# Accumulating across PSUM bank pairs: the two row halves of the TensorE array swap banks halfway through a sum

## The chip, the cores and the metric

The kernel runs on 1 core of one Trainium2 chip. The metric is the device time of one execution in microseconds; lower is better. The kernel before was run three times (180.81, 182.23 and 182.66 us, median 182.23 us). One further execution was recorded by the hardware profiler; all rows of a profile in this text come from that one.

## What is computed

The reference is a sigmoid attention followed by a token-mixing MLP, for 8 batches, 12 heads, 448 positions and heads of 64:

```python
def _attn_ref(q, k, v):
    scores = scale * np.matmul(q, k.transpose(0, 1, 3, 2)) - np.log(S)
    attn = 1.0 / (1.0 + np.exp(-scores))
    return np.matmul(attn, v)
...
def _moe_ref(x, w_q, w_k, w_out):      # x: 8 x 448 x 768
    wq = x @ w_q                       # 448 x 64
    wk = x @ w_k                       # 448 x 64
    W_tok = scale * np.einsum('bsd,btd->bst', wq, wk)
    mixed = np.einsum('bst,btd->bsd', W_tok, x)
    return np.maximum(mixed, 0.0) @ w_out
```

The kernel never forms W_tok. It computes wk-transposed times x first (a 64 x 768 matrix for each batch) and then wq times that.

## The kernel before, in words

**Units of work.** The 96 pairs of batch and head are handled as 24 "quads" of four heads; three quads make one batch ("unit" u, 0 to 7). Everything is bf16 on TensorE and float32 in PSUM. PSUM has 8 banks, which the program takes singly or in pairs in the order that the string BANKS (L67) lists.

**Four tiles of the array.** Most matmuls use the 128 x 128 array as four 64 x 64 tiles that run side by side: two row halves (`y` or `g` or `h`, the upper or lower 64 partitions of the operands, thus which half of a contraction) times two column halves (`x`, the upper or lower 64 partitions of the result). A group of four such matmuls is what one step in the plan issues several times. Because the two row halves work at the same time, they write to different banks of a pair.

**The plan.** The order of all work is written out by hand as a string of letters, PLAN (L132), which the loop at L803 walks. Each letter issues one step, and each engine runs its own instructions in that order. The letters that matter:
- S (`scores`, L307): four matmuls of 448 columns for one of 168 blocks of keys into a bank pair; ScalarE then writes the sigmoid of both banks to one of 16 `at` buffers (L316).
- P (`values`, L326): four matmuls of 448 columns that add one such block to the attention output of a quad; after seven of them the result goes to the tile `xt` (L342, at the end or for R split between VectorE and ScalarE, L340).
- x, X (`tr_x`, L346): transposes of `xt` into `xn`, in 64 x 64 tiles (x, L371) or whole (X, L355).
- W, w, L, l (`mlp_wqk`, L389): six steps for each unit give wq and wk. W and w use the whole array and one bank (L408). L and l use the four tiles: row half y sums its half of the contraction into bank y over all 448 columns (L396), and at the end one bank is copied to a float32 tile (L403), then the other is added to it (L404). POOL copies wq to the other half of the partitions (L405 and L417, or ScalarE at L415).
- N (`mlp_wkn`, L419): wk is transposed. U, u, T, t (`mlp_tmp` L431, `mlp_tmp_tiled` L443): wk-transposed times x; the tiled form again has two half sums in two banks, a copy (L456) and an addition (L457).
- M, m, G (`mlp_mix`, L466): three steps for each unit, a ReLU into the tile `mx` (L461 on ScalarE, L463 on VectorE). For the middle four units (the pairs of units listed in TW, L129) the step issues eight matmuls of 256 columns (L476) and writes `mx` in a wider layout; for the others it issues four of 448 columns (L490).
- O, o, Q, I, i: the product with `w_out`. Two units make 7 chunks of 128 tokens, 28 chunks in all, and each chunk takes four steps. There are three forms. `out_chunk` (L585) uses the whole array, three matmuls of 384 columns in a step (L603); it serves 44 steps, among them the last 20. `out_halves` (L545) uses four tiles, 12 matmuls of 384 columns in a step (L562): one block of 64 tokens at a time, both halves of the contraction into two banks, then a copy (L567) and an addition (L568); 12 steps. `out_pair` (L510) uses four tiles too, 12 matmuls in a step (L522), 56 steps: row half y makes all of the sum for token block y in bank y, so nothing has to be added, but each row half needs all of `w_out` and of `mx` on its own 64 partitions. That is why `wout16` (L107) holds `w_out` twice, the second copy with the halves of the partitions exchanged, made by the steps C (12 DMAs on the SP queue, L848), and why TW has its own layout of `mx`.
- q, k, a to f, r, s, z: q and k are cast and transposed to the layout that S wants. POOL does most casts (L192, L209, L215) and the exchange of partition blocks for kind c (L161, L164, L167), VectorE the 32 x 32 transposes (L245, L269, L276). The order of casts and loads is the string ORDER (L688). 1 and 2 give a cast to VectorE or ScalarE. F is filler for TensorE at the start.

**Queues.** Loads of q, k and v and nearly all stores are issued by SP in order (L173, L179, L543, L576, L613). A load waits for one of 8 buffers, a store for its copy out of PSUM into one of 3 buffers `o` (L60).

**Waiting on TensorE.** Matmuls carry no waits on other matmuls. TensorE's only waits are on other engines: that a bank has been read, or that an operand is there.

## Time and profile before

| | us |
|---|---|
| median of three runs | 182.23 |
| the profiled execution: its own time | 181.22 |
| its span, first to last instruction | 179.4 |
| PE busy / DVE busy / ACT busy / POOL busy | 169.1 / 143.0 / 158.9 / 124.2 |

PE is TensorE's matmuls, PEld its weight loads, DVE VectorE, ACT ScalarE, POOL GpSimd, SP the engine whose queue issues most DMAs. The granted TensorE clock was 0.997 over the span. A matmul's row lasts from its first column to the arrival of its last result, and matmuls overlap each other, so that PE is shown as busy even where it could take more work. The chain of waits, which lists for each stretch only the piece that the next one had to wait for, shows how far apart the pieces really start.

### The profile page before, as it was taken

The page shows a single profiled execution, that of the slowest core. Times are in us where ns is not written, and L with a number is a line of the kernel's source. Part 1 is how long each engine was busy: PE and PEld are TensorE (multiplying, and loading weights), DVE is VectorE, ACT ScalarE, POOL GpSimd, SP SyncE. Part 2 cuts the span into 40 slices and gives each one's busy share as a digit, 9 for nine tenths or more (in the row PEclk, how much of TensorE's full clock was granted, in tenths as well). Part 3 has the DMA queues.
Part 4 walks back from the last instruction along what each step waited for, and adds up shares of the span by engine and source line. Part 5 has one row for each costly group of instructions (what it writes and reads, how often), then busy time and mean ns, then how long its engine had stood idle before and what let it go on. Part 6 is the DMA issues. An engine that isn't in the chain of part 4 may idle for free.

```text
span 179.4 us, 7848 instructions
## 1 busy us (share of the span) xinstructions
PE 169.1 (94%) x3412; PEld 115.5 (64%) x3412; DVE 143.0 (80%) x223; ACT 158.9 (89%) x208; POOL 124.2 (69%) x169
## 2 busy tenths in 40 slices
PE   7888899889999999999999999999999999999990
PEld 7334545444674555755667788787888788888560
DVE  3447899998988897989999989979799885868351
ACT  4699999999999999999999999999999989967310
POOL 1286899998999999999999989879979810010000
PEclk9999999999999999999999999999999999999998
DMA  5999999999999998899996999959597432505876
GB/s 166 338 398 391 326 383 377 285 305 365 335 309 406 334 287 280 249 319 384 306 325 174 303 313 302 331 207 274 130 325 219 115 89 49 137 4 128 207 195 175
DMA packets 24914, 47.29 MB, mean 264 GB/s; under 512 B 3888, under 2 KB 18480, under 8 KB 24880
## 3 DMA queue, kind: packets, MB, share of 16 engines
q1 hardware_dynamic: 23600, 44.64, 76.9%
q0 software_dynamic: 800, 1.18, 3.6%
q10 hardware_dynamic: 480, 0.98, 1.5%
q8 instruction: 26, 0.43, 1.0%
q14 instruction: 8, 0.07, 0.1%
HBM read 35.78 MB, written 11.01 MB: 261 GB/s over the span
## 4 chain that ended last, share of the span: by engine, by line
PE 76%; ACT 15%; DMA 4%; SPq 1%; issue 1%; POOL 1%; DVE 0%
PE banks L311 16%; ACT at L316 15%; PE banks L522 15%; PE banks L333 14%; PE banks L603 13%; DMA k<-in_k_dram 4%; PE banks L562 3%; PE banks L408 3%; PE banks L371 2%; PE banks L396 2%; PE banks L355 2%; PE banks L452 2%; PE banks L476 1%; PE banks L490 1%; PE banks L437 1%
## 5 line engine op out<-in xcount | busy, mean ns | idle before, releaser
L316 ACT ACTIVATE at<-banks 128x896 bf16<-128x896 f32 x168 | 139.9, 951 | 2.9 <-PE banks L311 2.3
L311 PE MATMUL banks<-qk 64*64 64x448 bf16 x672 | 62.6, 357 | 3.7 <-ACT at L316 1.7
L333 PE MATMUL banks<-at,v 64*64 64x448 bf16 x672 | 47.3, 350 | 0.7 <-ACT at L316 0.7
L311 PEld LDWEIGHTS <-qk 64*64 64x64 bf16 x672 | 26.3, 105 | 21.4 <-issue 13.5
L522 PE MATMUL banks<-wout,mx 64*64 64x384 bf16 x672 | 36.3, 323 | 0.0
L333 PEld LDWEIGHTS <-v 64*64 64x64 bf16 x672 | 24.8, 106 | 6.7 <-issue 1.8
L342 DVE CAST xt<-banks 128x896 bf16<-128x896 f32 x22 | 23.7, 1083 | 2.4 <-PE banks L333 2.0
L522 PEld LDWEIGHTS <-mx 64*64 64x64 bf16 x672 | 23.2, 107 | 3.9 <-issue 0.2
L603 PE MATMUL banks<-wout,mx 128*128 128x384 bf16 (+1 forms) x138 | 24.4, 320 | 0.0
L192 POOL CAST qk<-k 128x896 bf16<-128x896 f32 x19 | 22.7, 1194 | 1.4 <-DMA k<-in_k_dram 1.0
L192 POOL CAST qk<-q 128x896 bf16<-128x896 f32 x18 | 21.5, 1193 | 2.5 <-DVE qk L276 1.4
L463 DVE TENSOR_SCALAR mx<-banks 128x1024 bf16<-128x1024 f32 (+3 forms) x22 | 21.3, 970 | 1.9 <-PE banks L476 0.7
L209 POOL CAST v<-v 128x896 bf16<-128x896 f32 x22 | 20.6, 950 | 1.4 <-DMA v<-in_v_dram 0.9
L603 PEld LDWEIGHTS <-mx 128*128 128x128 bf16 x138 | 12.3, 98 | 9.7 <-issue 3.2
L161 POOL COPY swap<-qk 32x448 uint32<-32x448 uint32 x28 | 15.5, 554 | 2.3 <-DVE qk L192 0.7
L276 DVE STREAM_TRANSPOSE qk<-qk 128x448 f32<-128x448 f32 x28 | 17.0, 628 | 0.1
L164 POOL COPY qk<-qk 32x448 uint32<-32x448 uint32 x28 | 15.8, 566 | 1.6
L167 POOL COPY qk<-swap 32x448 uint32<-32x448 uint32 x28 | 15.4, 552 | 1.6
L245 DVE STREAM_TRANSPOSE qk<-qk 32x448 f32<-32x448 f32 x24 | 15.3, 636 | 0.6
L405 POOL COPY wq<-wqk 64x448 bf16<-64x448 bf16 x3 | 1.7, 554 | 15.7 <-DVE wqk L404 15.7
L636 DVE COPY o<-banks 128x384 f32<-128x384 f32 x12 | 6.6, 554 | 5.7 <-PE banks L603 5.3
L636 ACT COPY o<-banks 128x384 f32<-128x384 f32 x9 | 4.4, 490 | 7.1 <-PE banks L603 6.6
(87 smaller groups left out, 207.9 us busy)
## 6 DMA issues: line engine op xcount, KB each, us to landing
q<-in_q_dram SPq DMA_DIRECT2D x24, 448.0 KB, 6.6
v<-in_v_dram SPq DMA_DIRECT2D x24, 448.0 KB, 6.6
k<-in_k_dram SPq DMA_DIRECT2D x23, 448.0 KB, 7.6
out_dram<-o SPq DMA_DIRECT2D x50, 192.0 KB, 4.2
wout<-in_moe_w_out_dram POOLq DMA_DIRECT2D x2, 576.0 KB, 11.7
wout<-wout SPq DMA_DIRECT2D x12, 96.0 KB, 5.6
out_dram<-o ACTq DMA_DIRECT2D x4, 192.0 KB, 3.2
k<-in_k_dram SPq DMA_DIRECT2D x1, 256.0 KB, 4.8
```

The costliest lines, as they stand in the source:

```text
L161: eng.tensor_copy(out=z[lo], in_=w[hi, 0])
L164: eng.tensor_copy(out=w[hi, 0], in_=w[lo, 1])
L192: COPY[e](out=f[:, :, "qk".index(nm)].rearrange("p e i d y -> p e y i d"), in_=ld.pop((nm, n)).rearrange("p (y i e d) -> p e y i d", y=2, ...
L209: COPY[e](out=t16.rearrange("p b i d -> p (b i d)"), in_=ld.pop((nm, n)).rearrange("p b x -> p (b x)"),)
L276: nc.vector.transpose(out=qk[n][:, t].rearrange("p t i n -> p (t i n)").bitcast(F32), in_=w)
L311: nc.tensor.matmul(sc[HALF[h], g, 0:S], qk[n][HALF[g], h, 1, i, :], qk[n][HALF[g], h, 0].rearrange("p i n -> p (i n)"), start=True, stop=True,
L316: inst = nc.scalar.activation(at, sc[:, :, 0:S], ACTF.Sigmoid, bias=attn_bias, scale=attn_scale)
L333: nc.tensor.matmul(ps[HALF[g], h, 0:S], ld["v16", n][HALF[h], g, i, :], ats[n, i][HALF[h], g, :], start=(i == 0), stop=(i == NI - 1),)
L342: read(fb, COPY[eng](out=xt(u, j)[:, :, 0:S], in_=ps[:, :, 0:S]))
L463: inst = nc.vector.tensor_scalar(dst, ps, moe_scale, 0.0, ALU.mult, ALU.max)
L522: nc.tensor.matmul(ps[HALF[x], y, 0:NB], mx[HALF[y], u, b, 64 * (i - 3 * y) : 64 * (i - 3 * y) + 64], wout16[HALF[y], slot(y, b), x * NB : ...
L603: nc.tensor.matmul(ps, mxs[w][:, 2 * S * c + m * P : 2 * S * c + (m + 1) * P], wout16[:, c, w0:w1], start=(c == 0), stop=(c == NC - 1),)
```

## The change

- `wout16` holds `w_out` once; the steps C and their 12 DMAs are gone. `out_pair` and the TW forms of `mlp_mix` and `mx` are gone: every mix step issues four matmuls of 448 columns, and every chunk in tiles goes through `out_halves`.
- `out_halves` no longer adds. One bank pair holds a chunk of two token blocks. In the steps with part 0 and 1 row half y sums its half of the contraction for token block y in bank y. In parts 2 and 3 the halves have changed: row half y goes on with the other token block in the other bank, adding to what the other half left there. One copy (or a pair of copies on VectorE and ScalarE, letter J) takes both banks out.
- `mlp_wqk` in tiles does the same with the two halves of the 448 columns, in twice as many matmuls of 224 columns; step j of the first three takes both blocks of quad j, so step 2 already needs the unit's last quad. `mlp_tmp_tiled` does it with the two halves of 384 columns, in twice as many matmuls of 192, and its second half is a step of its own (V; for an untiled unit V does nothing).
- Between the two halves `change` puts a nop on TensorE's queue that waits for the last matmul before the change.
- 20 `at` buffers in place of 16, 4 `o` buffers in place of 3.
- The strings BANKS, PLAN and ORDER are all new. By letters the new plan has 72 output steps in tiles (18 chunks) and 40 whole ones (before 68 and 44), 18 tiled W steps (3 units) as before, 4 tiled units in T and 4 untiled (before 5 and 3), 9 X and 15 x (before 10 and 14), 13 quads of kind c and 7 of kind r (before 14 and 6).

```diff
-    p_o = pool("o", 3)
+    p_o = pool("o", 4)
...
+    SYNC = mybir.DependencyInfo(mybir.DependencyClass.Sync, mybir.DependencyReason.DATA)
+    turned = {}
+
+    def change(key):
+
+        tc.add_manual_dep(
+            nc.tensor.nop().ins, turned.pop(key).ins.name, SYNC, reason="the halves of the array change banks",
+        )
...
-    wout16 = singles.tile([P, 2 * NC, D], BF16, name="wout16")
+    wout16 = singles.tile([P, NC, D], BF16, name="wout16")
...
-    at_bufs = [singles.tile([P, 2, S], BF16, name=f"at{n}") for n in range(16)]
+    at_bufs = [singles.tile([P, 2, S], BF16, name=f"at{n}") for n in range(20)]
...
-    TW = (1, 2,)
...
+        w, w2 = wqks[u % 2], wq2s[u % 2]
         if tiled:
-            for y in range(2):
-                for x in range(2):
-                    nc.tensor.matmul(
-                        ps[HALF[x], y, 0:S], wqk16[HALF[y], c, 64 * x : 64 * x + 64],
-                        xt(u, c // 2)[HALF[y], c % 2, 0:S], start=(c == 0), stop=(c == NC - 1),
-                    )
+
+
+            z, j = divmod(c, NJ)
+            if c == NJ:
+                change("W")
+            for b in (2 * j, 2 * j + 1):
+                for y in range(2):
+                    for x in range(2):
+                        inst = nc.tensor.matmul(
+                            ps[HALF[x], y ^ z, 0 : S // 2], wqk16[HALF[y], b, 64 * x : 64 * x + 64],
+                            xt(u, j)[HALF[y], b % 2, (y ^ z) * S // 2 : (y ^ z) * S // 2 + S // 2],
+                            start=(z == b == 0), stop=(z == 1 and b == NC - 1),
+                        )
+            if c == NJ - 1:
+                turned["W"] = inst
             if c == NC - 1:
-                w, w2 = wqks[u % 2], wq2s[u % 2]
-                part = p_one.tile([P, S], F32, tag="wpart", name="wpart")
-                read(fb, COPY["s" if act else "v"](out=part, in_=ps[:, 0, 0:S]))
-                read(fb, nc.vector.tensor_tensor(out=w[:, 0:S], in0=ps[:, 1, 0:S], in1=part, op=ALU.add))
-                nc.gpsimd.tensor_copy(out=w2[HALF[1]], in_=w[HALF[0], 0:S])
+                src = ps[:, :, 0 : S // 2]
+                read(fb, nc.vector.tensor_copy(out=w[:, 0:S].rearrange("p (z s) -> p z s", z=2), in_=src))
+                if tail or act:
+                    read(fb, nc.scalar.copy(out=w2[HALF[1]].rearrange("p (z s) -> p z s", z=2), in_=src[HALF[0]]))
+                else:
+                    nc.gpsimd.tensor_copy(out=w2[HALF[1]], in_=w[HALF[0], 0:S])
...
-            w, w2 = wqks[u % 2], wq2s[u % 2]
...
-    def mlp_tmp_tiled(u, act):
-        tmps[u] = p_one.tile([P, NB], BF16, tag="tmp", name="tmp")
-        part = p_one.tile([P, NB], F32, tag="upart", name="upart")
-        fb, ps, _ = bank2()
+    def mlp_tmp_tiled(u, t, act):
+        h = NB // 2
+        if t == 0:
+            tmps[u] = p_one.tile([P, NB], BF16, tag="tmp", name="tmp")
+            pt[0] = bank2()
+        else:
+            change("T")
+        fb, ps, _ = pt[0]
+
         for m in range(4):
             for r in range(2):
                 if 2 * m + r == NI:
                     continue
+                z = r ^ t
                 for y in range(2):
-                    nc.tensor.matmul(
-                        ps[HALF[y], r, 0:NB], wkn[u][HALF[r], m, :], xns[u][HALF[r], m, y * NB : (y + 1) * NB],
-                        start=(m == 0), stop=(m == 3 - r),
+                    inst = nc.tensor.matmul(
+                        ps[HALF[y], z, 0:h], wkn[u][HALF[r], m, :],
+                        xns[u][HALF[r], m, y * NB + z * h : y * NB + z * h + h],
+                        start=(t == m == 0), stop=(t == 1 and m == 3 - r),
                     )
-        read(fb, COPY["s" if act else "v"](out=part, in_=ps[:, 0, 0:NB]))
-        read(fb, nc.vector.tensor_tensor(out=tmps[u], in0=ps[:, 1, 0:NB], in1=part, op=ALU.add))
+        if t == 0:
+            turned["T"] = inst
+            return
+        read(fb, COPY["s" if act else "v"](
+            out=tmps[u].rearrange("p (z x) -> p z x", z=2), in_=ps[:, :, 0:h],
+        ))
...
-            mxs[w] = p_mx.tile([P, 2 * 12 * 256], BF16, tag="mx", name="mx")
+            mxs[w] = p_mx.tile([P, 12 * S], BF16, tag="mx", name="mx")
...
-        if w in TW:
-            for z in range(2):
-                for y in range(2):
-                    for x in range(2):
-                        nc.tensor.matmul(
-                            ps[HALF[x], y, 256 * z : 256 * z + 256],
-                            tmps[u][HALF[y], c * P + 64 * z : c * P + 64 * z + 64],
-                            wq[y][HALF[y], 192 * x : 192 * x + 256], start=True, stop=True,
-                        )
-            mx = mxs[w].rearrange("p (u y c x) -> p u c y x", u=2, y=2, c=3)[:, u % 2, c]
-            if tail:
-                for y in range(2):
-                    relu(fb, mx[:, y], ps[:, y], y)
-            else:
-                relu(fb, mx, ps, act)
-            return
...
-        mx = mxs[w][:, 0 : 12 * S].rearrange("p (y c u s) -> p c u y s", y=2, c=3, u=2)[:, c, u % 2]
+        mx = mxs[w].rearrange("p (y c u s) -> p c u y s", y=2, c=3, u=2)[:, c, u % 2]
...
-    def slot(half, b):
-
-        return b // 2 + (0 if b % 2 == half else NC)
-
-    def out_pair(act, split):
-
-        if opened:
-            w, blocks, part, fb, ps = opened.pop()
-        else:
-            w, blocks = chunks.pop(0)
-            part = 0
-            fb, ps, _ = bank2()
-        mx = mxs[w].rearrange("p (u b x) -> p u b x", u=2, b=12)
-        for b in range(3 * part, 3 * part + 3):
-            for y, (u, i) in enumerate(blocks):
-                for x in range(2):
-                    nc.tensor.matmul(
-                        ps[HALF[x], y, 0:NB], mx[HALF[y], u, b, 64 * (i - 3 * y) : 64 * (i - 3 * y) + 64],
-                        wout16[HALF[y], slot(y, b), x * NB : (x + 1) * NB],
-                        start=(b == 0), stop=(b == 11),
-                    )
-        if part < 3:
-            opened.append((w, blocks, part + 1, fb, ps))
-            return
-        o = p_o.tile([P, 2, NB], F32, tag="o", name="o")
-        if split:
-            for y in range(2):
-                read(fb, COPY["vs"[y]](out=o[:, y], in_=ps[:, y, 0:NB]), keep=True)
-        else:
-            read(fb, COPY["s" if act else "v"](out=o, in_=ps[:, :, 0:NB]), keep=True)
...
-            nc.sync.dma_start(out=dst, in_=o[HALF[x]])
-
-    def out_halves(act):
+    def out_halves(act, split):
...
-            ot[0] = p_o.tile([P, 2, NB], F32, tag="o", name="o")
-        o = ot[0]
-        b, h = divmod(part, 2)
-        if not h:
             fb, ps, _ = bank2()
+
+        z, h = divmod(part, 2)
+        if part == 2:
+            change("O")
         for c in range(3 * h, 3 * h + 3):
-            t0 = 2 * S * c + m * P + b * NP
             for y in range(2):
+                t0 = 2 * S * c + m * P + (y ^ z) * NP
                 for x in range(2):
-                    nc.tensor.matmul(
-                        ps[HALF[x], y, 0:NB], mxs[w][HALF[y], t0 : t0 + NP], wout16[HALF[y], c, x * NB : (x + 1) * NB],
-                        start=(c == 0), stop=(c == NC - 1),
+                    inst = nc.tensor.matmul(
+                        ps[HALF[x], y ^ z, 0:NB], mxs[w][HALF[y], t0 : t0 + NP],
+                        wout16[HALF[y], c, x * NB : (x + 1) * NB],
+                        start=(part == 0 and c == 0), stop=(z == 1 and c == NC - 1),
                     )
-        if h:
-            read(fb, COPY["s" if act else "v"](out=o[:, b], in_=ps[:, 0, 0:NB]), keep=True)
-            read(fb, nc.vector.tensor_tensor(out=o[:, b], in0=ps[:, 1, 0:NB], in1=o[:, b], op=ALU.add), keep=True)
+        if part == 1:
+            turned["O"] = inst
         if part < 3:
             opened.append((w, m, part + 1, fb, ps))
             return
+        o = p_o.tile([P, 2, NB], F32, tag="o", name="o")
+        if split:
+            for b in range(2):
+                read(fb, COPY["vs"[b]](out=o[:, b], in_=ps[:, b, 0:NB]), keep=True)
+        else:
+            read(fb, COPY["s" if act else "v"](out=o, in_=ps[:, :, 0:NB]), keep=True)
...
-        elif kind == "C":
-            for y in range(2):
-                nc.sync.dma_start(out=wout16[HALF[y], NC + c, :], in_=wout16[HALF[1 - y], c, :])
...
         elif kind == "U":
-            (mlp_tmp_tiled if t in "Tt" else mlp_tmp)(c, t in "ut")
+            tiled[c] = t if t in "Tt" else None
+            if tiled[c]:
+                mlp_tmp_tiled(c, 0, False)
+            else:
+                mlp_tmp(c, t == "u")
+        elif kind == "V":
+            if tiled[c]:
+                mlp_tmp_tiled(c, 1, tiled[c] == "t")
...
-                if u // 2 in TW:
-                    chunks.extend((u // 2, ((u % 2, i), (u % 2, 6 - i))) for i in range(3))
-                    if u % 2:
-                        chunks.append((u // 2, ((0, 3), (1, 3))))
-                else:
-                    chunks.extend((u // 2, m, -1) for m in (range(3, NI) if u % 2 else range(3)))
+                chunks.extend((u // 2, m, -1) for m in (range(3, NI) if u % 2 else range(3)))
...
-            if (opened or chunks)[0][0] in TW:
-                out_pair(t == "o", t == "Q")
-            elif t in "Ii":
-                out_halves(t == "i")
+            if t in "IiJ":
+                out_halves(t == "i", t == "J")
             else:
-                out_chunk(t in "oQ", tail)
+                out_chunk(t == "o", tail)
```

More of the change, by code (lines that the diff above doesn't have):

```diff
@@ L384, in tr_x @@
             read(fb, COPY["vs"[g] if tail else eng](out=dst, in_=src))
-    wkn, tmps, mxs = {}, {}, {}
+    wkn, tmps, mxs, pt = {}, {}, {}, {}
     pw = {}
@@ L702 @@
     ORDER = [(x[0], int(x[1:])) for x in ORDER.replace(".", "").replace("*", "").lower().split()]
-    done = dict.fromkeys("SPqkKxWNUMOCgz", 0)
+    done = dict.fromkeys("SPqkKxWNUVMOgz", 0)
     used, loaded, cast = set(), set(), set()
@@ L797 @@
     pump()
-    ALIKE = dict(a="q", c="q", e="q", r="q", b="k", d="k", f="k", s="k", j="k", h="k", X="x", y="x", Y="x", g="g", z="z", L="W", l="W", T="U", t="U", I="O", i="O", Q="O", G="M", R="P")
+    ALIKE = dict(a="q", c="q", e="q", r="q", b="k", d="k", f="k", s="k", j="k", h="k", X="x", y="x", Y="x", g="g", z="z", L="W", l="W", T="U", t="U", I="O", i="O", J="O", G="M", R="P")
     done["q"] = done["k"] = 1
-    quads_r = []
+    quads_r, tiled = [], {}
     for t in PLAN:
```

29 lines of the change are left out of this document (11 added, 18 removed), and 30 rows, old and new, of tables (BANKS, ORDER).

## Prediction

> **What bounds the kernel now.** I read the stretches first (busy time by stage), then the waits, then the chain of waits. Columns of the stretches: length, then busy us (count) of PE, PEld, DVE, ACT, POOL, then clock, DMA share and GB/s.
>
> ```profile
> 0.00:39.20 39.20, 33.64 (x577) 18.84 (x578) 28.88 (x53) 35.15 (x45) 28.39 (x39) 1.00 1.00 330
> 39.20:160.00 120.80, 120.29 (x2640) 85.76 (x2641) 105.48 (x155) 117.71 (x152) 95.79 (x130) 1.00 0.81 258
> 160.00:175.20 15.20, 15.19 (x201) 10.87 (x194) 8.31 (x16) 6.01 (x12) 0.00 (x0) 1.00 0.64 160
> ```
>
> From 39.2 us on PE has an instruction under way in 120.29 of 120.80 us and then in 15.19 of 15.20, at full clock. ACT is close behind (117.71, so 3.1 us free); DVE and POOL have 15 and 25 us free. The waits and the chain say where the first stage ends:
>
> ```profile
> PE banks L311 <- ACT at L316: 1.7, 6, 0.4
> ```
>
> ```profile
> 11.49 27.67 ACT at L316 x34
> ...
> 165.31 9.88 PE banks L603 x66
> ```
>
> ```profile
> 37.53 1.63 ACT at L316 x2
> 39.16 0.04 issue
> 39.20 0.38 PE banks L311 x4
> ```
>
> From 11.49 to 39.16 us the chain is nothing but sigmoids: ScalarE sets the pace, and PE waits for banks. At 39.20 us the 42nd S starts, and from there to 175.2 us the chain is matmuls, one behind the other. So two numbers decide: when that 42nd S can start, and how much TensorE must do after it. Work taken from DVE, POOL or the DMA queues is worth nothing by itself.
>
> **The price of a step.** The chain gives the distance between steps, which a mean duration does not, since matmuls overlap:
>
> ```profile
> 100.40 0.45 PE banks L355 x8
> 100.85 0.50 PE banks L311 x8
> 101.35 0.49 PE banks L522 x12
> 101.84 0.03 PE banks L423 x2
> ...
> 101.90 0.07 PE banks L423 x5
> ...
> 102.45 0.19 PE banks L311 x4
> 102.64 0.57 PE banks L452 x14
> ...
> 107.57 0.57 PE banks L333 x12
> 108.13 0.22 PE banks L476 x8
> ```
>
> ```profile
> 57.12 0.77 PE banks L437 x8
> ...
> 60.48 0.59 PE banks L603 x3
> 61.08 0.57 PE banks L408 x3
> ...
> 63.01 0.49 PE banks L603 x3
> ```
>
> ```profile
> 155.63 0.19 PE banks L490 x4
> ...
> 156.19 0.19 PE banks L396 x4
> 156.38 0.25 PE banks L371 x32
> ```
>
> S, P, W (whole or tiled) and the plain mix step cost 0.19 us, an output step 0.49 in either form, the TW mix step 0.22, X 0.45, x 0.25, N 0.10, T 0.57. Three L603 matmuls cost 0.59 right behind tiled work and 0.49 behind their like; two S behind whole work 0.50 instead of 0.38. So a change between tiles and whole array costs 0.10 to 0.12; I take 0.11 each, and U at 0.77 - 0.11 = 0.66.
>
> **Check on the old plan.** After the 42nd S its letters hold 311 steps of 0.19 (127 S, 133 P, 42 W, 9 plain mixes) = 59.1; 112 output steps = 54.9; 12 TW mixes 2.6; 7 N 0.7; 7 X 3.2; 13 x 3.3; 5 T 2.9; 2 U 1.3; 45 mode changes 5.0: together 132.8 us. The stretch took 175.2 - 39.2 = 136.0, so 3.2 us were lost to waits between steps.
>
> **The change, part by part.**
>
> *Stream and mode changes.* The new letters, counted in the same way: 322 steps of 0.19 (127 S, 132 P, 42 W, 21 mixes) = 61.2; 112 output steps 54.9; N, X and x as before 7.1; 4 T 2.3; 3 U 2.0; 46 mode changes 5.1: together 132.5, or -0.3 us. Losing `out_pair` costs nothing here: 0.49 us goes to 12 matmuls of 384 columns in both tiled forms. What it saves is 12 x (0.22 - 0.19).
>
> *The halved matmuls.* Tiled W and T issue twice as many matmuls of half the columns. The nearest row is L476, eight matmuls of 256 columns in 0.22 us: as many column cycles as 4 of 512, no more. I count the halves at the price of the whole.
>
> *The wait of TensorE on itself.* New, 25 times: 18 chunks, 3 W, 4 T. The trace shows none, so I build one. A matmul's result is there later than its slot ends (mean ns is the second number behind the bar), then a semaphore must travel, and the next weights were not loaded ahead:
>
> ```profile
> L522 PE MATMUL banks<-wout,mx 64*64 64x384 bf16 x672 | 36.3, 323 | 0.0
> L522 PEld LDWEIGHTS <-mx 64*64 64x64 bf16 x672 | 23.2, 107 | 3.9 <-issue 0.2
> L396 PE MATMUL banks<-xt,wqk 64*64 64x448 bf16 x72 | 5.1, 350 | 0.0
> ```
>
> ```profile
> 161.01 0.81 PE L452 MATMUL banks<-xn,wkn 64*64 64x384 bf16 x14
> ...
> 161.86 0.48 ACT L456 COPY upart<-banks 128x384 f32<-128x384 f32 x1 [0.81 <-PE banks L452]
> ...
> 162.38 0.56 DVE L457 TENSOR_TENSOR tmp<-banks,upart 128x384 bf16<-128x384 f32 x1
> ...
> 162.99 0.11 PEld L490 LDWEIGHTS <-tmp 64*64 64x64 bf16 x4
> ```
>
> 350 - 190 = 160 ns is the tail of a matmul (323 - 163 = 160 too). PE to ACT took 161.86 - 161.82 = 0.04 us, DVE back to PE 162.99 - 162.94 = 0.05. Weights not loaded ahead cost between 0 and 0.107; I take 0.10, since the array would be empty. Sum: 0.16 + 0.09 + 0.10 = 0.35 us from the end of the last old slot to the first new one. Other steps stand in between, and they cover it. By the new letters: 14 of 18 chunks have 0.38 us or more there (S and a mix step, two P), one has N and x (0.35), three have S and N (0.29); two W have over 0.7, the last only x (0.25); two T have 0.68, two a single S (0.19). Uncovered: 3 x 0.06 + 0.10 + 2 x 0.16 = 0.6 us. Ends: 0, and 25 x 0.35 = 8.8 us if nothing covers. I take 0.6, because the new letters put at least one step into every such place. Queued behind the waiting nop are all of TensorE's later steps, and ACT waits for their S; its `at` lead of up to 20 blocks and 3.1 us of slack bear that.
>
> The Trainium skill (PSUM — Partial Sum Buffer, Engine vs sequencer instructions) says that a nop is executed by the sequencer itself, a class apart from matmuls. No run here shows one on TensorE; by that, weights and matmuls behind it might be held back longer than behind a waiting matmul, which is the second rival below.
>
> *An operand due earlier.* Tiled W needs the unit's last quad in its third step, not its fifth. In the body other work lies between; for the last unit there is little:
>
> ```profile
> 155.63 0.57 PE L333 MATMUL banks<-at,v 64*64 64x448 bf16 x8
> ...
> 156.39 0.61 DVE L340 CAST xt<-banks 128x448 bf16<-128x448 f32 x1
> ```
>
> From the start of the last P: 0.35 for its results, 0.04, 0.61 for the copy, 0.05 back = 1.05 us. Covered by P and four steps of 0.19 = 0.95. Cost +0.1.
>
> *Additions, copies, DMAs.* Gone are these rows, 8.0 us of DVE, and the copies to float32 ahead of them:
>
> ```profile
> L568 DVE TENSOR_TENSOR o<-banks,o 128x384 f32<-128x384 f32 x6 | 3.3, 558 | 0.9 <-ACT o L567 0.4
> L457 DVE TENSOR_TENSOR tmp<-banks,upart 128x384 bf16<-128x384 f32 x5 | 2.8, 557 | 0.1
> L404 DVE TENSOR_TENSOR wqk<-banks,wpart 128x448 bf16<-128x448 f32 x3 | 1.9, 625 | 0.6 <-ACT wpart L403 0.3
> ```
>
> PE covers all of that, so 0 on the path; so are the 12 DMAs, the buffers, and one quad less of kind c on POOL. ACT gains some 0.5 us by its letters (three more splits of `xt`, one cast less) and keeps over 2 us free. If PE's cover were gone, DVE's saving would count where a bank waits for its copy.
>
> *The order.* At the 42nd S the old plan has 132.8 us of steps still ahead, the new one 132.5, so the crossing from ScalarE's pace to TensorE's stands where it stood; before it the sigmoids are the limit in both. I take the losses between steps as unchanged, 3.2 us. Ends: 0 and twice that; the only row of what an order loses is the old one, and I see no reason for more on one side.
>
> **The sum.** -0.3 + 0.6 + 0.1 = +0.4 us. The profiled execution took 181.22 us (span 179.4, 1.8 around it), so 181.6 on its scale. The median of the runs is 182.23, 1.0 higher; I predict 182.6 for the median.
>
> **The rivals.**
> 1. *As summed, about even*: 182.6, with 181.0 to 184.2 as its own range (losses or waits off by half).
> 2. *The wait is not covered*: the nop keeps weights and matmuls from being queued, and each of the 25 costs 0.15 us more: +3.8, 186.4. For it: 25 places, all on the bounding engine. Against: waits on other engines restart PE within 0.05 us. It decides (1.8 us, over 1%) from 0.06 us each.
> 3. *The new order waits more*: banks or operands come late, losses 3.2 to 6: +2.8, 185.4. For it: every bank is assigned anew, and a tiled chunk still holds its pair for four steps. Against: DVE and POOL have less to do.
> 4. *Faster*: lighter DVE and earlier free banks take the losses from 3.2 to 0.8: -2.4, 180.2. It needs 2.2 of the 3.2 us to pass 1%. Against: only a few waits name DVE, and after 60 us PE hardly idles.
> 5. *Weight loads show*: W and T load twice as often, 18 + 14 = 32 more groups of four at 0.107: +3.4, 186.0. The L476 row speaks against it: two groups of loads within 0.22 us that 512 columns fill anyway. The Trainium skill (TensorE: Matmul & The Clock Gate, The mechanism) lets a load overlap running matmuls only in another row group; both row halves load here, so that rule would have it, and the trace does not agree.
>
> **How the numbers follow.** Chances: first 0.55, second 0.20, third 0.12, fourth 0.09, fifth 0.04. Over and under 1% is about what a measurement of this kernel can tell from no change. Faster 0.09; within 1% 0.55; slower 0.20 + 0.12 + 0.04 = 0.36. The range 180.3 to 186.2 takes in the first, third and fifth case and parts of the others.
>
> **What would show it.** Right: the chain after about 39 us is matmuls again, the same stretch from the 42nd S takes 136 to 137 us, and behind a part 2 the gap is under 0.1 us. L404, L457 and L568 gone and DVE some 8 us lighter with no gain in time. Wrong: gaps of 0.2 us or more ahead of each second half (rival 2); PE waits on DVE, POOL or banks (3); tiled W steps over 0.22 us (5); the first S of each quad later than before.

## The result and the profile after

| | before | after |
|---|---|---|
| median of the runs made for the comparison, us | 182.10 (22 runs, 180.79 to 184.69) | 182.94 (22 runs, 181.51 to 183.93) |
| profiled execution: own time, span, us | 181.22, 179.4 | 183.3, 181.5 |
| DVE busy, us | 143.0 | 137.6 |

The ratio after to before is 1.0061, with a 95% interval of 1.0036 to 1.0086: about 0.8 us more on the medians, 0.6 per cent by the ratio. (Ratios are formed without disturbed runs, so they need not be the quotient of two medians.) The forecast was 182.6 and "within 1%".

The busy line of the page of the changed kernel, then its stretches (columns as in the prediction):

```profile
PE 170.4 (94%) x3546; PEld 114.0 (63%) x3546; DVE 137.6 (76%) x217; ACT 157.7 (87%) x206; POOL 120.5 (66%) x163
```

```profile
0.00:39.20 39.20, 34.00 (x604) 18.96 (x605) 27.27 (x50) 35.14 (x45) 28.58 (x40) 1.00 0.97 340
39.20:162.00 122.80, 121.19 (x2740) 85.47 (x2739) 101.89 (x153) 118.05 (x154) 91.93 (x124) 1.00 0.77 245
162.00:177.20 15.20, 15.17 (x214) 9.51 (x202) 8.12 (x15) 4.54 (x9) 0.00 (x0) 1.00 0.54 134
```

The first stretch and the last 15 us look as before. The middle one is 2.0 us longer, and PE now stands idle for 1.6 us of it, where it was 0.5 us. The timeline has the 42nd S (L319), the chain the last matmuls (L583):

```profile
38.99 0.38 PE L341 MATMUL banks<-at,v 64*64 64x448 bf16 x4 [0.40 <-POOL v L217]
39.20 0.38 PE L319 MATMUL banks<-qk 64*64 64x448 bf16 x4
```

```profile
167.30 9.88 PE banks L583 x66
```

The 42nd S starts at 39.20 us, as before, and the stretch from there to the end of the matmuls has grown from 136.0 to 138.0 us. Less the prediction's priced steps (132.8 and 132.5), the losses between steps went from 3.2 to 5.5 us. Where do 2.3 us come from? The chain of the changed kernel names two places at once:

```profile
123.65 0.48 PE banks L536 x11
124.13 0.67 issue
124.80 0.32 PE banks L536
...
142.36 0.18 PE banks L319 x3
142.54 0.74 issue
143.28 0.35 PE banks L319
```

"issue" is time in which the engine waited for nothing that the profile shows. Both stops lie inside a step: between the 11th and 12th matmul of an output step, and between the third and fourth of an S. The profile names no missing operand or bank there. The kernel before has one of them, also inside a step (chain):

```profile
53.80 0.15 PE banks L311
53.96 0.35 issue
```

Counted in the trace, all three stand at the same place: behind row 193 of a block of 256 rows of TensorE (matmuls and weight loads, and two other rows at the start). The changed kernel's 7098 rows (7092 matmuls and weight loads, 6 others) make nearly 28 such blocks, and the queue for instructions moved 27 packets, 0.44 MB, so some 16 KB each. Each stop ended 1.3 to 1.5 us after the latest of these packets had landed. So these look like late instructions. A program's text doesn't show them. Shorter ones stand at 137.18 us after and at 121.0 before, with 0.11 and 0.08 us idle. Together TensorE is idle for 0.67 + 0.74 + 0.11 = 1.5 us after and 0.35 + 0.08 = 0.4 before. A matmul's own duration hides the start of each stop: from one matmul's start to the next the gaps are 0.99, 1.09 and 0.46 us after, 0.70 and 0.27 before. So the stops are 1.1 to 1.6 of the 2.0 us between these two executions, and they say nothing about the medians. For those, experiments were needed.

The theories, as the expectations name them: the stops at instruction blocks (FETCH); late operands and banks in the new order of all steps (ORDER, later in a narrower form LATE, with NEXT against it); the waits of TensorE on itself; the new sums (SUMS).

### The profile page after: what moved, and what is told of

Same layout as the page of the kernel before. It is cut to its first block, busy times and chain, and to the rows that moved or that the text cites. A ratio compares the mean times of both kernels' runs of the same rounds, so it can differ in the third digit from the quotient of the medians.

```text
span 181.5 us, 8089 instructions
## 1 busy us (share of the span) xinstructions
PE 170.4 (94%) x3546; PEld 114.0 (63%) x3546; DVE 137.6 (76%) x217; ACT 157.7 (87%) x206; POOL 120.5 (66%) x163
## 4 chain that ended last, share of the span: by engine, by line
PE 75%; DMA 12%; POOL 6%; issue 2%; SPq 1%; DVE 1%; POOLq 0%; DVEq 0%
PE banks L536 20%; PE banks L319 15%; PE banks L341 15%; PE banks L583 11%; DMA w<-in_moe_w_k_dram 4%; DMA v<-in_v_dram 4%; DMA k<-in_k_dram 3%; POOL qk L200 3%; PE banks L427 3%; PE banks L503 2%; PE banks L379 2%; PE banks L363 2%; PE banks L411 2%; PE banks L455 1%; POOL v L217 1%
## 5 line engine op out<-in xcount | busy, mean ns | idle before, releaser
L319 PE MATMUL banks<-qk 64*64 64x448 bf16 x672 | 62.9, 357 | 3.1 <-ACT at L324 1.1
L536 PE MATMUL banks<-wout,mx 64*64 64x384 bf16 x864 | 46.3, 324 | 0.7 <-issue 0.7
L319 PEld LDWEIGHTS <-qk 64*64 64x64 bf16 x672 | 26.8, 105 | 19.5 <-issue 10.8
L536 PEld LDWEIGHTS <-mx 64*64 64x64 bf16 x864 | 28.4, 106 | 7.6 <-issue 1.6
L341 PEld LDWEIGHTS <-v 64*64 64x64 bf16 x672 | 23.2, 106 | 9.5 <-POOL v L217 2.2
L492 DVE TENSOR_SCALAR mx<-banks 128x896 bf16<-128x896 f32 (+1 forms) x23 | 20.5, 904 | 5.1 <-PE banks L503 4.9
L200 POOL CAST qk<-q 128x896 bf16<-128x896 f32 x20 | 23.8, 1192 | 0.7 <-DMA q<-in_q_dram 0.2
L350 DVE CAST xt<-banks 128x896 bf16<-128x896 f32 x18 | 19.6, 1086 | 4.0 <-PE banks L341 3.6
L583 PE MATMUL banks<-wout,mx 128*128 128x384 bf16 (+1 forms) x126 | 21.7, 319 | 0.0
L253 DVE STREAM_TRANSPOSE qk<-qk 32x448 f32<-32x448 f32 x28 | 17.8, 636 | 0.7
L583 PEld LDWEIGHTS <-mx 128*128 128x128 bf16 x126 | 11.3, 98 | 8.9 <-issue 2.7
L551 DVE COPY o<-banks 128x768 f32<-128x768 f32 x11 | 10.5, 951 | 4.9 <-DMA out_dram<-o 1.8
L392 DVE COPY xn<-banks 128x1024 bf16<-128x1024 bf16 (+1 forms) x15 | 9.8, 651 | 1.9 <-PE banks L379 1.7
```

The costliest lines, as they stand in the source:

```text
L200: COPY[e](out=f[:, :, "qk".index(nm)].rearrange("p e i d y -> p e y i d"), in_=ld.pop((nm, n)).rearrange("p (y i e d) -> p e y i d", y=2, ...
L253: nc.vector.transpose(out=qk[n][other : other + 32, h].rearrange("p t i n -> p (t i n)").bitcast(F32), in_=w[own : own + 32, 1 - h],)
L319: nc.tensor.matmul(sc[HALF[h], g, 0:S], qk[n][HALF[g], h, 1, i, :], qk[n][HALF[g], h, 0].rearrange("p i n -> p (i n)"), start=True, stop=True,
L341: nc.tensor.matmul(ps[HALF[g], h, 0:S], ld["v16", n][HALF[h], g, i, :], ats[n, i][HALF[h], g, :], start=(i == 0), stop=(i == NI - 1),)
L350: read(fb, COPY[eng](out=xt(u, j)[:, :, 0:S], in_=ps[:, :, 0:S]))
L492: inst = nc.vector.tensor_scalar(dst, ps, moe_scale, 0.0, ALU.mult, ALU.max)
```

## The experiments

**The changed kernel again.**

> The changed kernel once more, for a second profile and more rounds. Theory FETCH: TensorE's two long stops in the first profile (0.67 us inside the output step at 123.45 us, 0.74 us inside the S at 142.17 us) end no wait on another engine; they stand 193 rows behind a multiple of 256 rows of TensorE, 1.3 to 1.5 us behind the end of a 16 KB instruction transfer, so they are instruction blocks that came late, and how late differs from run to run. Then the stops of the second profile stand at other multiples of 256 rows or have other lengths (0 to 1.1 us each). Theory ORDER: they belong to these two steps (a bank or an operand that the new order brings late), so the same two steps show 0.6 us or more again. Time by both: 0.3 to 1.0% over the kernel before.

Measured: 183.08 us (12 runs), ratio 1.0064 (1.0023 to 1.0105), span 180.5. In this execution the stretch from the 42nd S (39.46 us) took 136.7 us, against 138.0 in the first, and the long stops are gone (one of 0.64 us from start to start, at 137.08). That one stands at the same matmul as the stop at 137.18 us in the first profile. So where a stop can come is given by the program's blocks of 256 rows; whether it comes and how long it is differs between executions. The median stays 0.8 us above the kernel before even so.

**64 nops ahead, to shift the blocks.**

```diff
+    for _ in range(64):
+        nc.tensor.nop()
```

> The changed kernel with 64 nops on TensorE's queue in its idle time at the start, so that every block of 256 instructions ends 64 instructions earlier in the plan; nothing else differs. FETCH: long stops that end no wait appear only where the row number, with the 64 nops counted, is 193 above a multiple of 256, thus 129 above one in the rows without them; none at the two steps of the first profile unless by a wait. ORDER: the stops stay at the output step of chunk (1, 6) and at block 5 of quad 21. Time: FETCH from -0.8 to +0.8 us against the changed kernel, since other steps now meet the late blocks; ORDER within 0.2 us of it.

Measured: 182.93 us (12 runs), ratio 1.0019 (0.9975 to 1.0062). The nops left no rows, and the stops still came behind row 193 of each 256, among them one of 1.5 us at 126.23 us. As a shift of the blocks the test is void; it is one more run of the same plan. The stop of 1.5 us stands at the same matmul as the one after 124.13 us in the first profile; the stop at 142.54 us there is missing here, and another came (0.33 us from start to start, at 135.72 us).

**No load traffic, both kernels.** The loads after the first eight bring 64 of 896 columns, so most of the data of q, k and v is left out.

```diff
+        small = len(held) > 8
...
+        if small:
+            eng.dma_start(out=dst[:, 0, 0:64], in_=src[:, 0, 0:64])
```

> The kernel before with nearly no load traffic: the first eight loads as they are, each later load of q, k or v brings 64 of its 896 columns into a buffer that still holds old data (so the output is another one; all other work is the same). FETCH: the instruction transfers no longer queue among loads, so TensorE's stops at row 193 above a multiple of 256 shrink below 0.1 us each, and the time falls by what they cost, 0.5 to 1.5 us. If nothing depended on the load traffic: the same time within 0.3 us.

> The changed kernel in the same way. FETCH together with the late output weights: it falls by 1 to 3 us, and its distance to the kernel before in the same way is -0.3 to +0.5 us. ORDER or WAITS (the new order or the 25 waits themselves cost the time): the distance stays at +0.8 to +1.2 us.

Measured: the kernel before 180.46 us (9 runs), ratio 0.9908 (0.9869 to 0.9948); the changed one 181.37 (10 runs), ratio 0.9951 (0.9917 to 0.9986), both to the unaltered kernel before. The long stops are gone from both traces, and each kernel gains about as much as the other: by the ratios 0.9 per cent before, and 1.1 after (from 1.0061 to 0.9951). The distance between the plans stays: 0.9 us. The gain of the kernel before, 1.7 us by its ratio, is more than FETCH foresaw (0.5 to 1.5) and more than the stops of its own profile. The spread shrinks too: the kernel before takes 180.20 to 181.27 us without loads, 180.79 to 184.69 with them. So the load traffic makes much of the spread, but not the difference of the medians. That it does so through late instructions fits but isn't shown run by run: of the eleven traces of this case with full loads six have a stop with 0.28 us idle or more, five have none of that length, and the three without most of the loads have none at all. What is left between the two kernels is in the plan. The ends of the two traces, from the timelines (42nd S) and chains (last matmuls), before and then after:

```profile
39.75 0.38 PE L333 MATMUL banks<-qk 64*64 64x448 bf16 x4
```

```profile
165.07 9.89 PE banks L625 x66
```

```profile
39.03 0.38 PE L341 MATMUL banks<-qk 64*64 64x448 bf16 x4 [0.33 <-DVE xt L372]
```

```profile
165.03 9.89 PE banks L605 x66
```

That is 135.2 and 135.9 us: losses of 2.4 and 3.4 us over the priced steps, 1.0 us more in the new plan, in one execution of each. Counted matmul by matmul at the same prices, the new plan has lost 1.0 us more than the old by 50 us. Half of that the old plan loses as well by 70 us, and the new one adds as much again behind that, in smaller pieces. The largest single place is at 46.6 us. TensorE and VectorE there, changed kernel without its loads (timelines):

```profile
46.61 0.38 PE L341 MATMUL banks<-qk 64*64 64x448 bf16 x4
47.30 0.52 PE L498 MATMUL banks<-xn,wkn 64*64 64x192 bf16 x14 [0.31 <-DVE wkn L469]
47.58 0.43 PE L341 MATMUL banks<-qk 64*64 64x448 bf16 x4
47.88 0.52 PE L498 MATMUL banks<-xn,wkn 64*64 64x192 bf16 x14
48.30 0.57 PE L341 MATMUL banks<-qk 64*64 64x448 bf16 x8
49.05 0.55 PE L385 MATMUL banks<-ident,xt 128*128 128x128 bf16 x7 [0.18 <-DVE tmp L506]
```

```profile
45.70 1.39 DVE L222 CAST qk<-ld 128x896 bf16<-128x896 f32 x1
46.98 0.27 DVE L469 COPY wkn<-banks 128x256 bf16<-128x256 bf16 x1
```

From the S at 46.61 to the one at 48.49 there are three S and two half T, 3 x 0.19 + 2 x 0.285 = 1.14 us of work (half a T at half the price of a T); they took 1.88. The first T waits for the copy `wkn`, which VectorE does behind a cast of 1.39 us; X waits for the copy `tmp`.

**The wait alone, in the kernel before.** Its 14 chunks in `out_pair` get the same nop ahead of part 2.

```diff
+        if part == 2:
+            change("O")
...
+        if part == 1:
+            turned["O"] = inst
```

> The kernel before, in its own order, with one part of the change alone: TensorE's wait on the last matmul of part 1 ahead of part 2, in the 14 chunks of the paired form (no bank changes, nothing else is removed). Nine of them have one S between, the others more. With 0.35 us for a wait, as predicted: 9 x 0.16 + 0.06 + 0.10 = +1.6 us. With the 0.225 us that the bare waits measured: 9 x 0.035 = +0.3 us. If a wait costs nothing beyond: 0.

Measured: 182.45 us (12 runs), ratio 1.0013 (0.9972 to 1.0054). By the interval, 14 waits with other steps in between cost between -0.5 and +1.0 us; that they cost something isn't shown.

**The wait with nothing in between.** The changed kernel, with part 1 of each tiled chunk moved behind the steps that stood between it and part 2.

```diff
+                if part == 2 and tiles:
+                    moved = steps.pop(first)
+                    steps.append(moved)
```

> The changed kernel with the steps between part 1 and part 2 of each of the 18 tiled chunks issued ahead of part 1, so that nothing covers TensorE's wait on itself. As predicted, an uncovered wait costs 0.35 us: 18 x 0.35 = +6.3 us against the changed kernel, less 0.2 us that the three thin covers cost already. By the gaps in the changed kernel's trace (0.06 to 0.07 us from the end of the last matmul to the first one behind the wait, with 0.16 us of tail before it) it costs 0.22 to 0.23: 18 x 0.225 = +4.0 us. If the wait were no real stop, under +1 us.

Measured: 192.58 us (4 runs), ratio 1.0576 (1.0506 to 1.0647). The view of waits (us in total, times, the longest) and the timeline at one of them:

```profile
ACT at L343 <- PE banks L338: 10.3, 20, 0.9
...
PEld L555 <- PE banks L555: 7.9, 18, 0.4
```

```profile
50.96 1.43 PE L555 MATMUL banks<-wout,mx 64*64 64x384 bf16 x24
...
51.71 0.47 PEld L555 LDWEIGHTS <-mx 64*64 64x64 bf16 x16 [0.44 <-PE banks L555]
```

All 18 waits are there. They stand on the next weight load; the nop itself has no row. Across the wait two groups of four matmuls start 0.38 to 0.395 us apart where 0.163 is usual: a bare wait costs 0.226 us. Eighteen make 4.1 of the 9.6 us. The rest came with the new places of the steps (ScalarE now waits 10.3 us for S), so the total says less about the wait than its own rows.

**The sums with copies and additions, in the new order.** The W and T of the changed kernel go back to two half sums, a copy and an addition (T still issued in two steps); its chunks keep the change of banks. The edit of W at its end:

```diff
+                part = p_one.tile([P, S], F32, tag="wpart", name="wpart")
+                read(fb, COPY["s" if act else "v"](out=part, in_=ps[:, 0, 0:S]))
+                read(fb, nc.vector.tensor_tensor(out=w[:, 0:S], in0=ps[:, 1, 0:S], in1=part, op=ALU.add))
```

> The changed kernel with W and T back at two half sums and an addition, in the new order: 7 of the 25 waits and 128 of 3546 matmuls (and as many weight loads) gone, 3 copies and additions of wq and wk and 4 of the tmp tile back on VectorE or ScalarE. By the prediction's sum: -0.5 us (uncovered waits of 0.10 and 2 x 0.16), by the gaps of the trace -0.1 us; FETCH gives up to 0.5 us more, as one block of 256 instructions fewer is needed; if the additions hold anything up, +0.5 us or more.

Measured: 184.44 us (6 runs), ratio 1.0125 (1.0069 to 1.018), 1.1 us above the changed kernel by the ratios, 1.4 by the medians. All six runs lie above all but one of the changed kernel's 34. TensorE now waits for the additions (timeline; L468 adds `tmp`, L412 adds `wqk`):

```profile
72.46 0.44 PE L379 MATMUL banks<-ident,xt 64*64 64x64 bf16 x30 [0.38 <-DVE tmp L468]
...
163.22 0.22 PE L430 MATMUL banks<-ident,wqk 64*64 64x64 bf16 x2 [0.46 <-DVE wqk L412]
```

So the new order counts on the shorter sums. Leaving out the additions is worth 1.1 to 1.4 us in this order, though no wait of TensorE in the profile of the kernel before names them.

**The new sums in the old order.** The kernel before with the changed W and T (the second half of each T one or two steps behind the first), and with the wait in `out_pair`; it keeps the second copy of the output weights.

> The kernel before in its own order, with its second copy of the output weights, but with the changed sums: the tiled W and T change banks halfway (no half copies, no additions; the second half of each tiled T one or two steps behind the first), and the wait ahead of part 2 of its output chunks too, as in the kernel with that wait alone (182.45, ratio 1.0013). Theory ORDER (the self-waits and the sums cost next to nothing wherever they stand, and the changed kernel's 0.9 us come with its new order of all steps): 182.1 to 182.6, ratio 0.999 to 1.003; VectorE about 5 us less busy than in the kernel before, and no time gained by it. Rival SUMS (the halved weight loads, the operands that the second half needs earlier, or the waits cost the 0.9 us themselves): 182.8 to 183.3, ratio 1.004 to 1.007. If the additions were on the path after all in the old order: 181.6 or less.

Measured: 183.71 us (12 runs), ratio 1.0099 (1.0064 to 1.0134); 1.3 us above the kernel with the wait alone by the medians, 1.6 by the ratios. Both expectations were too low. TensorE at one of the five T, in the kernel with the wait alone and then in this one:

```profile
103.15 0.82 PE L459 MATMUL banks<-xn,wkn 64*64 64x384 bf16 x14
103.76 0.40 PE L318 MATMUL banks<-qk 64*64 64x448 bf16 x4
```

```profile
103.06 0.51 PE L475 MATMUL banks<-xn,wkn 64*64 64x192 bf16 x14
103.67 0.38 PE L318 MATMUL banks<-qk 64*64 64x448 bf16 x4
103.85 0.68 PE L552 MATMUL banks<-wout,mx 64*64 64x384 bf16 x12
104.34 0.52 PE L475 MATMUL banks<-xn,wkn 64*64 64x192 bf16 x14
```

The S behind the T can't start before ScalarE has read its bank: 0.61 us after the start of T, with a whole T or with half of one. A whole T (0.57 us) fills that time. Half a T, 0.28 us where nothing holds the next step up, leaves 0.3 us of it empty, and its other half comes on top later. That costs 0.2 to 0.3 us at four of the five T, by the starts of the S around them in the two traces. The last unit's W adds some 0.4, because its third step now needs the last quad:

```profile
158.92 0.39 PE L410 MATMUL banks<-xt,wqk 64*64 64x224 bf16 x8 [0.23 <-DVE xt L347]
```

Together this is about the 1.3 us. So the changed sums make the old plan slower, at least with the second half of T in these places; the old sums make the new plan slower; and the two belong together.

**Weights and operands earlier, in the new order.** First the output weights ahead of k7 and v4 on GpSimd, since in the repeat of the changed kernel TensorE waited for them at 50.9 us:

```diff
-        "... W5 k7 v4 w1 w4 q7 v5 q8 ..."
+        "... W5 w1 w4 k7 v4 q7 v5 q8 ..."
```

> The changed kernel with the two loads of the output weights issued on POOL ahead of the casts of k7 and v4 rather than behind them, about 2.1 us earlier. In two profiles of the changed kernel the second output step waits 0.4 to 0.8 us for them, in the first it does not. LATE WEIGHTS: -0.3 to -0.6 us against the changed kernel, and no wait of an output step for them. If the stop were hidden by later slack, or k7 and v4 then come late: 0 to +0.5 us.

Measured: 184.96 us (6 runs), ratio 1.0128 (1.0075 to 1.0181), 1.2 us above the changed kernel by the ratios, 2.0 by the medians: outside both ranges. The wait for the weights is gone, but GpSimd's other work is late, and the 42nd S starts at 42.15 us:

```profile
35.34 0.38 PE L503 MATMUL banks<-wq,tmp 64*64 64x448 bf16 x2 [0.86 <-POOL wq L435]
...
37.45 0.96 PE L341 MATMUL banks<-at,v 64*64 64x448 bf16 x8 [1.17 <-POOL v L217]
```

Then v5 ahead of q7, for the wait of 0.40 us at 38.99 shown above; then, besides, a cast on VectorE moved from ahead of the copy `wkn` to behind the first T; then both without the load traffic:

```diff
-        "... k7 v4 w1 w4 q7 v5 q8 ..."
+        "... k7 v4 w1 w4 v5 q7 q8 ..."
...
-        "...1NPPPSTSVSScX..."
+        "...NPPPST1SVSScX..."
```

> The changed kernel with one pair of entries of the cast and load order swapped (v5 ahead of q7), so that GpSimd casts v5 about 1.2 us earlier; in the changed kernel TensorE stood 0.68 us at 38.99 us (0.61 in its repeat) for exactly this cast. Theory LATE (what the change loses beside the instruction blocks is operands that the new order brings late around the crossing, and an earlier cast gives its wait back): the 42nd S starts 0.4 to 0.7 us earlier (at 38.5 to 38.9 us) and the median is 0.4 to 0.7 us under the changed kernel's 182.94, 182.2 to 182.6. Rival NEXT (the next operand is late in its place: q7, the sigmoids of ScalarE, or a bank): the 42nd S is no earlier than 39.1 us, a wait for another engine stands within 2 us behind it, and the median stays within 0.2 us of 182.94.

> As the kernel with v5 ahead of q7, and the one cast of a k that VectorE does at 45 to 46 us (1.39 us) moved from ahead of the copy of the second unit's folded weights to behind the first half of its tiled T, so that this copy isn't queued behind it. Without the load traffic the changed kernel's TensorE stood 0.66 us from start to start (0.31 us idle) there. Theory LATE: the two gains add, 0.3 to 0.6 us more, so the median is 0.7 to 1.3 us under 182.94: 181.6 to 182.2, about before's. Rival NEXT: the gap at the tiled T closes but the cast's 1.39 us now holds VectorE's copy of tmp or xt, and TensorE waits for that: within 0.2 us of the kernel with v5 ahead alone.

> The same two moves, in the changed kernel whose later loads bring 64 of 896 columns (so it leaves out most of the data of those loads): no stops for instruction blocks, so what the order costs shows alone. That kernel took 181.37, and the kernel before without its loads 180.46. Theory LATE: 180.3 to 180.9, that is, two thirds of the 0.9 us between the two plans come back. Rival NEXT: 181.2 to 181.5, unchanged; then the 0.9 us are spread over waits that follow from the whole order and not from these two late operands.

Measured: 182.05 us, ratio 1.002 (0.9982 to 1.0058); 182.91, ratio 1.0033 (0.9994 to 1.0071); 181.52, ratio 0.9964 (0.9938 to 0.9991); 12 runs each. The first can't be told apart from the kernel before, nor surely from the changed one. Its median is 0.9 us under the changed kernel's, more than LATE foresaw and against NEXT; but with the second move besides it is 182.91 again, which neither theory foresaw. So these two medians decide nothing. In the trace of the first TensorE no longer waits for v5, and still the 42nd S starts at 39.50 us, as NEXT said: the next operand holds it.

```profile
38.79 0.38 PE L341 MATMUL banks<-at,v 64*64 64x448 bf16 x4
...
39.50 0.38 PE L319 MATMUL banks<-qk 64*64 64x448 bf16 x4 [0.33 <-DVE xt L350]
```

Without loads the two moves bring nothing (181.52 against 181.37; NEXT had 181.2 to 181.5). The trace shows why: T no longer waits, and X waits longer. TensorE, then VectorE:

```profile
46.84 0.52 PE L498 MATMUL banks<-xn,wkn 64*64 64x192 bf16 x14
...
49.18 0.61 PE L385 MATMUL banks<-ident,xt 128*128 128x128 bf16 x8 [0.57 <-DVE tmp L506]
```

```profile
48.02 0.68 DVE L222 CAST qk<-ld 128x896 bf16<-128x896 f32 x1
48.58 0.55 DVE L506 CAST tmp<-banks 128x384 bf16<-128x384 f32 x1
```

At the prediction's prices the losses between 40 and 50 us are 1.4 us, as in the kernel without the moves (1.3). For these two moves LATE fell and NEXT held. But the moved cast now stands right ahead of the copy `tmp` on VectorE, so the wait of X may be the cast's own doing; a plan with this cast off VectorE wasn't tried.

None of the kernels that do the whole work was shown to be faster than the kernel before.

## Why the prediction was right, step by step

**The crossing at 39.2 us: right in number, wrong as a picture.** The 42nd S came at 39.20 us in both profiled executions. But the prediction took it for the point where ScalarE stops being a limit, with 3.1 us free from there on. The stretches for ScalarE alone (length, busy us and count, clock, DMA share, GB/s), before and then after, say when that free time comes:

```profile
54.00:60.00 6.00, 5.66 (x8) 1.00 1.01 387
60.00:70.00 10.00, 9.66 (x14) 1.00 0.96 304
70.00:80.00 10.00, 10.00 (x14) 1.00 0.85 272
```

```profile
54.00:60.00 6.00, 6.00 (x9) 1.00 0.84 257
60.00:70.00 10.00, 9.90 (x13) 1.00 0.87 279
70.00:80.00 10.00, 9.59 (x12) 1.00 0.85 315
```

Ahead of 54 us ScalarE is full in both. Its first stop above 0.06 us comes at 54.6 us before and at 75.7 us after; by 70 us it has stood for 0.68 us before and 0.10 after. (Without the load traffic it is 61.7 us and, but for 0.08 us at 48.0, 75.9 us.) Up to there two engines are full at once. With 0.81 us for a sigmoid, TensorE can't go on for long there with less than about 0.81 us of steps for each S.

**Losses between steps unchanged, 3.2 us: this step failed.** Without the load traffic they are 2.4 and 3.4 us, 1.0 more, of which 0.3 belong to two terms below (waits 0.2, operand 0.1). So the order loses some 0.7 us more, where the prediction saw no reason for a difference. The largest place is the one shown at 46.6 us: three S with 1.14 us of work, where three sigmoids take 2.43, and T and X wait for VectorE's copies. Why the order loses there is argued, not shown. For a lack of other work speaks that the kernel before gives any three S between the 42nd and the 57th at least 1.85 us of it, and that the wait only moved when its operand came earlier. Against it speaks that the kernel before gives three S from the 58th on 1.33 us, and without loads takes 1.40 for them. VectorE's work ahead of the two copies remains as a rival. It wasn't tried with other work put in, nor with the cast off VectorE. So the third rival (operands come late) had the right mechanism at a quarter of its 2.8 us.

**The waits, 0.6 us: the mechanism right, the size too high.** The term of 0.35 us for a round trip was built as 0.16 + 0.09 + 0.10. A bare one measures 0.226: 0.16 for the tail and 0.065 where the prediction had 0.19 for the way of the semaphore and the weights. In the changed kernel the second half starts 0.06 to 0.07 us behind the last result of the first at five places; at the others it starts later, behind the steps in between. What the 25 waits cost beyond these steps adds up to about 0.2 us at most; where S and N stand between (0.29 us) nothing shows. The second rival's condition, 0.06 us more at each of 25 places, didn't come. The prediction left open whether a nop holds back more than a waiting matmul. Here the wait stands on the next weight load, 0.44 us by its row, and the matmuls lose only the 0.226.

**Stream and mode changes, -0.3: it holds.** The same prices leave 132.5 us of steps, and the tiled halves keep to them. From the chain of the changed kernel, L411 a tiled W, L476 half a T:

```profile
120.50 0.19 PE banks L411 x8
...
122.59 0.38 PE banks L411 x16
...
131.55 0.25 PE banks L476 x12
```

Eight half matmuls take 0.19 us, as four whole ones did. Twelve of the 14 of half a T take 0.25, thus all 14 some 0.29, and two halves the 0.57 of a whole T. The doubled weight loads don't show, so the fifth rival is out.

**An operand due earlier, +0.1: right.** In the timeline of the changed kernel the copy of `xt` ends at 159.62 + 0.62 = 160.24 us, and the third W step starts 0.06 us behind it, 0.12 later than the mix step ahead of it leaves room for (159.99 + 0.19 = 160.18):

```profile
159.62 0.62 DVE L348 CAST xt<-banks 128x448 bf16<-128x448 f32 x1 [0.32 <-PE banks L341]
```

```profile
159.99 0.36 PE L503 MATMUL banks<-wqk,tmp 64*64 64x448 bf16 x2
...
160.30 0.39 PE L411 MATMUL banks<-xt,wqk 64*64 64x224 bf16 x8
```

In the old order the same edit cost 0.4 us at that place.

**Additions, copies and DMAs at 0: right against the kernel before, and too simple.** DVE is 5.4 us less busy (some 8 were foretold) and the time didn't fall. But in the new order the sums with additions cost 1.1 to 1.4 us. "Hidden" is a property of a plan, not of an operation.

**The sum.** Foretold +0.4 us: -0.3, +0.6, +0.1, 0. Found, without load traffic: -0.3 for the steps and +1.0 for losses (0.2 of waits on itself, 0.1 of the operand, 0.7 of the order), thus +0.7 in the stretch, and 0.9 in the medians. The sum came out close because the waits were priced 0.4 too high and the order 0.7 too low: that these nearly cancel is luck. The first two profiles, with spans 2.1 us apart, would have told a wrong story.

## What to carry to other kernels

Where two engines are full at once, reckon the work per unit of the slower one along the order, not only the sum behind a crossing point, and look there for what each step waits for. Bringing one operand forward may only move the wait to the next, as it did here. Before a sum is rewritten, ask what its length was covering; the changed sums were worth 1.1 to 1.4 us in one order and cost 1.3 or more in another. Two single profiles can differ by more than the change is worth: look for stops that name no releaser and run the same kernel twice.

## What the runs showed of the hardware

- TensorE stopped for up to 1.5 us, from one matmul's start to the next, with no releaser in the profile. Every such stop with 0.28 us idle or more, in six of the eleven traces with full loads, stands behind row 193 of 256 and ended 1.3 to 1.6 us after a 16 KB packet of the instruction queue had landed; the three traces without most of the loads have none. With full loads these packets start 68 to 90 rows behind the last such place in the median of a trace, without them 27 to 33. That the loads delay them fits, but wasn't tried by itself.
- A wait of TensorE on its own matmul, through a nop, leaves no row for the nop. It stands on the next weight load and costs 0.226 us bare; behind 0.29 us of other steps no cost shows.
- Weight loads for half matmuls on all four 64 x 64 tiles stay hidden: eight loads in a step of 0.19 us. The Trainium skill (TensorE: Matmul & The Clock Gate, The mechanism) says in a list that a load overlaps running matmuls "only when row_grp differs", though the sentences ahead of it also allow a load into a background weight buffer. This trace, with both row halves loading throughout, does not agree with the list; it doesn't speak against the second.
